# Another write pattern in a linear-attention readout, the first GLU opened tile by tile, and a new hand-written instruction order

## The chip, the cores and the metric

The kernel runs on one core of a Trainium2 chip. The metric is the device time of one execution in microseconds (us), as the median of several executions. A core has five engines with queues of their own: TensorE (PE in the profile, with its weight loads shown apart as PEld), VectorE (DVE), ScalarE (ACT), GpSimd (POOL) and SyncE (SP), which here only issues DMAs.

## What is computed

Four layers are applied to one sequence of 2048 tokens with 512 features, in bf16: attention A, GLU B, attention A, GLU B, each as `x = x + layer(layernorm(x))`, the two A layers with the same weights and the two B layers too. Cut to its core:

```python
def A(x, wqkv, w_phi, wo):                 # H = 32 heads of 16
    q, k, v = split_heads(x @ wqkv)
    pq, pk = q @ w_phi, k @ w_phi          # per head, 16 x 16
    phi_q = concat(softmax(pq), softmax(-pq))   # 32 features a head
    phi_k = concat(softmax(pk), softmax(-pk))
    kv = einsum("bhsf,bhsd->bhfd", phi_k, v)
    z  = einsum("bhsf->bhf", phi_k)
    num = einsum("bhqf,bhfd->bhqd", phi_q, kv)
    den = einsum("bhqf,bhf->bhq", phi_q, z)[..., None] + 1e-6
    return merge_heads(num / den) @ wo

def B(x, W_gate, W_up, W_down):            # F = 1376
    return (relu(x @ W_gate) * (x @ W_up)) @ W_down
```

## The kernel before

**Tiling.** The 2048 tokens are 16 tiles of 128 (`NT`), in four slabs of four. All weights and the whole of `x` stay in SBUF. `w_phi` is folded into the k and q weights at the start (`compose_k`, `compose_q`). The layers are called A0, B1, A2, B3 and the norms in front of them L0, L1, L2, L3.

**Attention.** For every tile, `kv_proj` or `kv_pair` (L670, L704) makes k and v and takes the exponentials. `knorm` (L689) sums them, takes the reciprocal and scales them. `kv_acc` (L721) adds `phi_k` times v into two banks of PSUM, with a column of ones beside each head's 16 values of v (`vsb[..., 16]`), so that z comes out in the same matmul. `kv_fin` (L737) copies the sums out with a mask: `kvf` for the feature-major readout, `kvbd` for the other.

**The two readouts.** In the first attention, tiles 0 to 3 have q in feature-major form (`q_fm`, L799), and `num_fm` (L813) reads them out. Eight matmuls a tile give the unnormalised result of both softmax signs, copies bring it to SBUF ("numcp"), and then come six small steps: `zm`, `zd`, `zr` (the reciprocal), `ab` (the factors), `tsc` (L845: all 1024 products) and `o` (L852: the sum of the two signs, 512 elements, written to `osb`). For tiles 0 and 1 the steps run on VectorE; for tiles 2 and 3 `zm`, `zd`, `ab` and `o` run on GpSimd. In `tsc` the order of a group's elements is feature, then head (`d h`); in `osb` it is head, then feature (`h d`), as the output projection wants it. All other tiles use `num` (L856), whose q goes through `qnorm` (L782) and two transposing DMAs.

**Behind the readout.** `out_proj` (L873) transposes `osb` (on PE for tiles 0 and 1, `PT`; by DMA for the others), multiplies by `wo`, and `resid` (L636) adds it to `x` with a running sum. `center` (L652) centres the tile for the next norm ("L1 apply") and transposes it ("L1 tr").

**GLU.** `glu_up` (L887) works on a list of tiles. It makes one piece for the last 96 of the 1376 hidden columns (`last`, "gu", L928, whose result goes through a transposing DMA, "htr") and ten pieces (`step`, L902) of 128 hidden columns: four matmuls for the gate, four for up, each with as many columns as the list has tokens. ScalarE takes the relu (L904); for some pieces it also copies up to SBUF (L910), and VectorE multiplies in SBUF (L912); for the others VectorE reads up from PSUM (L915). The pieces rotate through four banks of PSUM (0 to 3) and 18 places in `hT` (`NHU`). `glu_down` (L942) adds up a tile's eleven pieces and the residual (L953).

**What sets the order.** `emit` makes a list of all operations with what they read and write. `ORDER` gives for every engine the sequence in which it issues its operations, as positions in that list in base 36. Each engine runs its sequence strictly in that order and waits on semaphores where an operation needs another's result. `schedule` and `prepare` work out the waits from it; the duration that each operation carries in its call ("planner's duration") sets no wait on the chip by itself. SP's sequence holds nearly all DMAs, among them every transposing one.

Of the kernel before, what the change touches and what calls it, by code (L numbers as in the profile page):

```python
# [14 lines left out]
        "1i 1k 1j 1e 1h 1g 1f 1l 2e 47 2o 2y 3d 38 4r 3i 42 4c 4m 4w 3n 5n 5o 5b 67 66 5h 78 3s 7p 77 7o 91 92 6x 93 85 b8 b9 71 ba 8a cd ce a4 8f cf a8 8k di "  # L15
        "dj eb eh ec dk fb fc ei eo fd g9 ga en eu et gw gx la lb g8 gv lu hl hp lv il ip lk jl ll jp kd m5 m4 kh me mf mp mo o9 o8 nx ou ot oj p4 pe pf pp pz "
        "q0 qa if jf ql qk qv sw sx sl th t7 k7 kz ti uu ts v5 uv vf vg nm ws vq wt x3 z1 zd zc sa zn uj wh 110 zy zx 11b 11a 11l yi 11w 11v 12y 13j 139 138 "
        "10p 12n 178 14m 16x 16e 18a 17z 191 19c 19w 1ab 1b1 1a7 1bh 1cj 1bx 1an 1cl 1ck 1fj 1dl 1ax 1g8 1bd 1dj 1bt 1e9 1dk 1eb 1ea 1c9 1f0 1cx 1go 1ez 1f1 "
        "1hr 1h4 1gk 1jy 1g3 1hq 1hs 1ke 1ig 1if 1h0 1ku 1hg 1i4 1it 1iu 1ie 1la 1jh 1ju 1j6 1ji 1is 1ln 1lo 1ka 1kq 1mc 1jg 1mb 1l6 1lm 1n1 1n2 1m0 1ns 1ma "
        "1nr 1og 1n0 1oh 1ss 1sy 1pi 1pj 1nq 1to 1tn 1oj 1oi 1t4 1u2 1u1 1pl 1pk 1ta 1ug 1uf 1tm 1u0 1uu 1uv 1z0 1ue 1z1 1ut 1z2 1z3 1zf 1ze 1zd 1zo 1zc 1zp "  # L20
        "1zq 202 201 200 1zr 203 20d 20p 20o 20e 1wq 20r 20q 20c 20f 22a 22m 22b 21z 1xj 22w 22x 22l 1y4 238 237 1yp 23u 23i 23t 23j 24g 244 245 24f 24q 21o "
        "24r 251 252 275 276 26u 27h 26j 27g 27r 283 295 27s 282 296 29r 29h 29g 29s 2ad 2a3 2a2 2ae 2bh 2bg 2dt 2ds 2dh 28u 2ee 2b5 2e3 2e4 2ef 2eq 2ep 2ft "
        "2g3 2fs 2g4 2gf 2ge 2gq 2gp 2cy 2i3 2h0 2h1 2i4 2lm 2ly 2lx 2m8 2m9 2mk 2fh 2mv 2mu 2mj 2ny 2o8 2o9 2ok 2nx 2ou 2p6 2oj 2ov 2q8 2q9 2p5 2hs 2jl 2l3 "
        "2nm 2px 2rj 2ss 2t4 2t3 2tf 2tp 2te 2ub 2tq 2u0 2u1 2uc 2uy 2ux 2um 2un 2v9 2v8 2vv 2vj 2vk 2vu 2xp "),
    "dve": (
        "3x 25 26 2f 2g 29 4h 2p 2j 2q 2z 30 2t 33 4x 4z 4y 51 53 50 52 54 6j 6l 6k 6m 58 9r 9s 5p 5q 5e 68 69 6v 9t 9q 79 6z 7a 7q 7r 94 97 95 bb 98 a2 bc be "
        "bf cj a6 cg ck ch dl dm do dp fe fh ff gb fi gc gy ge gz mq h1 hf hb ha hd hc he hg hh hs ht hu hv hw hx is hy it iu iv i3 iw js ix i8 jv iy i9 jx j3 "
        "ie mr mx j8 j9 kk my je kn kp oa ny rl rm ok ov nc nd p5 k4 kw pg kx pq k5 s0 s1 qb tu q1 tv qm nj qw vs vt nk u9 r8 ua xt sm rk w7 w8 s7 s8 t8 sy tt "
        "tj ug xu uh 100 uw 101 v6 we wf vr vh wu 11y x4 11z 13x y8 13y y9 z2 zo 10f 15p ze 10g 15q 18c 18d 12d xg xs 12e 111 zz 17a 17b yf yg 10m 11c 14c 11m "
        "11x 14d 12z 10n 13k 12k 12l 13a 13w 164 165 14j 14k 150 17p 17q 15c 18r 18s 15o 16b 16c 19m 19n 16y 17w 1a9 18y 18z 17x 19t 19u 1fh 18b 179 1az 19d "  # L30
        "1g6 1a8 1ao 1bv 1bf 1be 1ay 1bu 1ca 1cy 1dm 1cm 1h2 1e0 1da 1jw 1cn 1ec 1ed 1g4 1gl 1gm 1ht 1dn 1hu 1f2 1eq 1hh 1kc 1ks 1h1 1f3 1ih 1ii 1fg 1l8 1i5 "
        "1j7 1iv 1iw 1jv 1kr 1kb 1lp 1jj 1lq 1l7 1jk 1md 1me 1m1 1n3 1n4 1nt 1mr 1nu 1sq 1ok 1nh 1ol 1sw 1pm 1pn 1o7 1t2 1tp 1or 1os 1p9 1t8 1tq 1u3 1u4 1pt "
        "1pu 1uh 1ui 1uk 1uw 1ux 1uz 1vy 1vz 1vw 1vx 20s 1w8 20t 1w9 20z 1x1 1we 210 1x2 1wj 1xu 1wk 1xv 1x7 1wp 1yf 1yg 1xc 1xd 21e 21f 1xi 285 25u 25v 220 "
        "1y1 1y2 1ym 22y 286 22c 22n 21l 21m 269 239 2ag 23v 1yn 23k 24h 26a 246 24s 2ah 253 28k 28l 25f 2es 2av 2aw 26v 26g 25s 27i 277 26h 28r 28s 2b2 284 "
        "2b3 27t 2et 297 29i 2c9 29t 2co 2af 2ca 2a4 2iw 2bi 2h3 2h4 2cp 2di 2du 2ke 2ix 2mx 2my 2f7 2f8 2eg 2kf 2bu 2er 2cv 2cw 2e5 2hi 2c7 2fu 2hj 2p8 2gg "
        "2fe 2ff 2gr 2g5 2p9 2jb 2jc 2hp 2hq 2h2 2i5 2ih 2kt 2ku 2ji 2jj 2ln 2kc 2lz 2iu 2nc 2nd 2ma 2pn 2po 2mw 2jz 2ml 2nj 2nk 2r9 2ra 2l0 2nz 2l1 2oa 2ol "
        "2ow 2qa 2p7 2qm 2pu 2pv 2rg 2rh 2st 2tg 2t5 2u2 2qz 2tr 2rx 2ud 2uo 2sa 2va 2uz 2vl 2vw 2w8 2wl 2wy 2xb 2xn "),
# [318 lines left out]
NT, NSLAB, NC, NFC = 16, 4, 4, 11  # L356
# [10 lines left out]
KVD = 31.0  # L367
# [6 lines left out]
class Kernel:  # L374
# [89 lines left out]
    def setup(self):  # L464
        op, dma, r = self.op, self.dma, self.r
        k = self
# [677 lines left out]
```

## Time and profile before

| what | value |
|---|---|
| median of six runs | 388.01 us |
| lowest and highest | 386.31 and 389.32 us |
| the profiled execution | 387.43 us |
| its span in the profile | 385.4 us |
| granted TensorE clock, mean over the span | 0.996 |
| instructions | 6623 |

The span is the time from the first to the last instruction that the profiler recorded; about 2.0 us of the profiled execution lie around it. In the profile a line such as L852 is a line of the kernel before. The word "busy" counts the time in which an engine has an instruction in work; matmuls overlap, so that a busy PE need not be one that streams at full rate. The chain that ended last is followed back from the last instruction, at each step to what released it.

### The profile page before, as it was taken

The page shows a single profiled execution, that of the slowest core. Times are in us where ns is not written, and L with a number is a line of the kernel's source. Part 1 is how long each engine was busy: PE and PEld are TensorE (multiplying, and loading weights), DVE is VectorE, ACT ScalarE, POOL GpSimd, SP SyncE. Part 2 cuts the span into 40 slices and gives each one's busy share as a digit, 9 for nine tenths or more (in the row PEclk, how much of TensorE's full clock was granted, in tenths as well). Part 3 has the DMA queues.
Part 4 walks back from the last instruction along what each step waited for, and adds up shares of the span by engine and source line. Part 5 has one row for each costly group of instructions (what it writes and reads, how often), then busy time and mean ns, then how long its engine had stood idle before and what let it go on. Part 6 is the DMA issues. An engine that isn't in the chain of part 4 may idle for free.

```text
span 385.4 us, 6623 instructions
## 1 busy us (share of the span) xinstructions
PE 366.8 (95%) x2416; PEld 200.1 (52%) x2459; DVE 260.9 (68%) x527; ACT 219.1 (57%) x433; POOL 161.4 (42%) x286
## 2 busy tenths in 40 slices
PE   5999987899999999999999999989999999999996
PEld 4555543576754445444444446566664444444443
DVE  4999889798868566346758697886766753441242
ACT  3899864753454307864656676975444623484540
POOL 7799932823354101713776777314037210103000
PEclk9999998999999999999999999999999999999999
DMA  7643950344535444400220124535534432231013
GB/s 244 155 81 59 281 227 0 70 80 97 89 66 84 96 95 84 82 3 0 56 41 0 25 44 58 83 69 82 79 73 97 82 80 57 71 69 41 2 27 123
DMA packets 92176, 30.37 MB, mean 79 GB/s; under 512 B 83984, under 2 KB 91120, under 8 KB 92144
## 3 DMA queue, kind: packets, MB, share of 16 engines
q1 hardware_dynamic: 90848, 28.84, 35.2%
q10 hardware_dynamic: 1296, 1.11, 1.0%
q8 instruction: 19, 0.31, 0.4%
q14 instruction: 13, 0.11, 0.1%
HBM read 7.91 MB, written 2.10 MB: 26 GB/s over the span
## 4 chain that ended last, share of the span: by engine, by line
PE 84%; DMA 5%; DVE 4%; ACT 3%; issue 1%; SPq 1%; ACTq 1%; POOL 1%; DVEq 0%
PE ps L902 35%; PE ps L951 18%; PE ps L677 9%; PE ps L882 7%; PE ps L711 4%; PE ps L767 3%; DMA oT<-osb 3%; PE ps L928 2%; PE ps L732 2%; DMA wv_p<-in_A_wqkv_dram 2%; PE ps L861 1%; ACT expq L772 1%; PE ps L807 1%; SPq L796 1%; DMA yT<-ytile 1%
## 5 line engine op out<-in xcount | busy, mean ns | idle before, releaser
L902 PE MATMUL ps<-yT,Wgu 128*128 128x512 bf16 (+1 forms) x788 | 148.0, 336 | 1.1 <-DVE h10t L933 0.5
L902 PEld LDWEIGHTS ps<-yT,Wgu 128*128 128x128 bf16 x800 | 75.6, 98 | 61.1 <-ACT expk L910 2.7
L904 ACT ACTIVATE gate_sb<-ps 128x512 bf16<-128x512 f32 (+1 forms) x100 | 49.6, 510 | 59.5 <-PE ps L902 34.7
L951 PE MATMUL ps<-Wd,hT 128*128 128x512 bf16 (+2 forms) x353 | 79.3, 372 | 0.6
L699 POOL TENSOR_TENSOR expk<-expk,rZk 128x1024 bf16<-128x1024 bf16 (+1 forms) x32 | 59.0, 1863 | 12.2 <-DVE rZk L694 12.2
L951 PEld LDWEIGHTS ps<-Wd,hT 128*128 128x128 bf16 (+1 forms) x363 | 34.8, 98 | 38.2 <-DMA hT<-h10t 0.5
L910 ACT ACTIVATE expk<-ps 128x512 bf16<-128x512 f32 (+1 forms) x65 | 32.0, 498 | 32.5 <-PE ps L902 30.1
L664 POOL TENSOR_SCALAR rv<-rv 128x1 f32<-128x1 f32 x48 | 8.8, 192 | 86.0 <-ACT sq L662 86.0
L912 DVE TENSOR_TENSOR hT<-gate_sb,expk 128x512 bf16<-128x512 bf16 (+1 forms) x65 | 24.8, 390 | 22.4 <-ACT gate_sb L904 14.3
L692 DVE TENSOR_REDUCE Zk<-expk 128x64 f32<-128x1024 bf16 x32 | 38.1, 1200 | 2.4 <-ACT expk L685 1.5
L915 DVE TENSOR_TENSOR hT<-gate_sb,ps 128x512 bf16<-128x512 bf16 (+1 forms) x35 | 20.9, 602 | 26.6 <-ACT gate_sb L904 14.8
L662 ACT ACTIVATE sq<-x_sb,nmr 128x512 bf16<-128x512 bf16 x48 | 34.6, 720 | 4.7 <-DVE x_sb L953 3.4
L785 DVE TENSOR_REDUCE Zq<-expq 128x64 f32<-128x1024 bf16 x28 | 33.7, 1205 | 4.4 <-ACT expq L772 2.9
L790 POOL TENSOR_TENSOR rho<-rZq,Zq 128x32 f32<-128x32 f32 x28 | 7.4, 267 | 68.9 <-DVE rZq L789 68.7
L953 DVE SCALAR_TENSOR_TENSOR x_sb<-ps,rstd,x_sb 128x512 bf16<-128x512 f32 (+1 forms) x33 | 23.4, 714 | 18.9 <-PE ps L951 15.3
L882 PE MATMUL ps<-wo_p,oT 128*128 128x512 bf16 x123 | 32.5, 386 | 3.3 <-DMA oT<-osb 2.5
L793 POOL TENSOR_TENSOR expq<-expq,rho 128x256 bf16<-128x256 bf16 x56 | 34.4, 629 | 1.6
L767 PE MATMUL ps<-Wqp,yT 128*128 128x512 bf16 x106 | 27.8, 386 | 0.5 <-issue 0.2
L639 DVE SCALAR_TENSOR_TENSOR x_sb<-ps,x_sb 128x512 bf16<-128x512 f32 x32 | 21.9, 685 | 7.5 <-PE ps L882 6.1
L677 PE MATMUL ps<-Wkp,yT 128*128 128x512 bf16 x86 | 22.6, 379 | 0.6 <-ACT Wkp L544 0.4
L868 DVE TENSOR_TENSOR osb<-ps,rden 128x512 bf16<-128x512 f32 x28 | 19.0, 680 | 5.2 <-DMA oT<-osb 4.7
L677 PE MATMUL ps<-wv_p,yT 128*128 128x512 bf16 x83 | 21.8, 379 | 0.8 <-DMA wv_p<-in_A_wqkv_dram 0.5
(116 smaller groups left out, 464.6 us busy)
## 6 DMA issues: line engine op xcount, KB each, us to landing
out_dram<-x_sb SPq DMA_DIRECT2D x15, 128.0 KB, 1.8
x_sb<-in_A_x_dram SPq DMA_DIRECT2D x3, 512.0 KB, 7.6
Wgu<-in_B_W_gate_dram SPq DMA_DIRECT2D x4, 344.0 KB, 6.6
Wgu<-in_B_W_up_dram SPq DMA_DIRECT2D x4, 344.0 KB, 6.6
Wd<-in_B_W_down_dram SPq DMA_DIRECT2D x5, 256.0 KB, 4.2
yT<-ytile SPq DMA_TRANSPOSE x56, 2.5
qT<-expq SPq DMA_TRANSPOSE x56, 2.5
x_sb<-in_A_x_dram SPq DMA_DIRECT2D x4, 128.0 KB, 3.6
```

What stands on the lines that cost most here:

```text
L662: op("act", lambda e: e.activation(k.sq[:], k.x_sb[:, t, :], ACT.Square, scale=-float(D), bias=k.nmr[:, t, :], accum_out=k.rv1[:, t, :]), ...
L677: op("pe", (lambda ic, bank, W: lambda e: e.matmul(k.pb[bank][:], k.yT[:, ic, t * 128:(t + 1) * 128], W[:, ic, :], start=(ic == 0), stop=( ...
L692: op("dve", lambda e: e.tensor_reduce(k.Zk[:, zb, :], k.expk[:, t, :, :, :].rearrange("p g s (h f) -> p (g s h) f", f=16), AX.X, ALU.add), ...
L699: op(eng, (lambda kv, u0, n: lambda e: e.tensor_tensor(kv, kv, k.rZk[:, rb, u0 * 32:u0 * 32 + n].unsqueeze(2).to_broadcast([P, n, 16]), AL ...
L767: op("pe", (lambda ic, bank, tt: lambda e: e.matmul(k.pb[bank][:], k.yT[:, ic, tt * 128:(tt + 1) * 128], k.Wqp[:, ic, :], start=(ic == 0), ...
L785: op("dve", lambda e: e.tensor_reduce(k.Zq[:, b, :], k.expq[:, t, :, :, :].rearrange("p g s (h f) -> p (g s h) f", f=16), AX.X, ALU.add), ...
L793: op("pool", (lambda ev, u: lambda e: e.tensor_tensor(ev, ev, k.rho[:, b, u * 16:u * 16 + 16].rearrange("p (g h) -> p g h", h=4).unsqueeze ...
L882: op("pe", (lambda c, bank: lambda e: e.matmul(k.pb[bank][:], k.oT[:, ob, c, :], k.wo_p[:, c, :], start=(c == 0), stop=(c == NC - 1)))(c, ...
L902: op("pe", (lambda bank, W, ic, fc, Mf: lambda e: e.matmul(k.pb[bank][0:Mf, 0:n], W[:, ic, fc * 128:fc * 128 + Mf], k.yT[:, ic, c0:c0 + n] ...
L904: op("act", (lambda Mf, gb, gs: lambda e: e.activation(k.gate_sb[0:Mf, gs, 0:n], k.pb[gb][0:Mf, 0:n], ACT.Relu))(Mf, gb, gs), [self.RP[gb] ...
L910: op("act", (lambda Mf, ub, up: lambda e: e.activation(up[0:Mf, 0:n], k.pb[ub][0:Mf, 0:n], ACT.Copy))(Mf, ub, up), [self.RP[ub]], ru, 170 ...
L951: op("pe", (lambda fc, Kf, u, c0, bank, m0, m1: lambda e: e.matmul(k.pb[bank][:, m0:m1], k.hT[0:Kf, u, c0:c0 + 128], k.Wd[0:Kf, fc, m0:m1] ...
```

## The change

Four things change in the code; the arithmetic stays the same.

1. The last add of the feature-major readout (`num_fm`, L850 to L852) goes through its elements in the order in which they lie in `osb`. It now writes neighbouring elements one after the other and reads both inputs at a step of 8 elements; before it read neighbouring elements and wrote at a step of 16.
2. In the first GLU, tiles 0 and 1 are worked on one after the other as lists of one tile each. Before they were one list of two. Tiles 2 and 3 stay a list of two, and the second GLU (`last`) is unchanged.
3. The column of ones in `vsb` is set by four fills, one for each slab, each with a resource of its own, instead of one fill.
4. All five sequences in `ORDER` are new, and some planner's durations.

```diff
-KVD = 31.0
+KVD = 33.0
...
-        op("pool", lambda e: e.memset(k.vsb[:, :, :, 16:17], 1.0), [], [r("vones")], 2270, "v ones")
+        for st in range(NSLAB):
+            op("pool", (lambda st: lambda e: e.memset(k.vsb[:, st * 4:st * 4 + 4, :, 16:17], 1.0))(st), [], [r("vones", st)], 620, f"v ones {st}")
...
-               [r("phik", t, bank), r("v", t), r("vones")], [self.RP[bank]], KVD, f"{tag} kvacc {t} {g}")
+               [r("phik", t, bank), r("v", t), r("vones", t // 4)], [self.RP[bank]], KVD, f"{tag} kvacc {t} {g}")
...
-        ov = k.osb[:, b, :].rearrange("p (c h d) -> p c d h", c=NC, h=8)
-        tv = k.tsc[b].rearrange("p (s c d h) -> p s c d h", s=2, c=NC, h=8)
+        ov = k.osb[:, b, :].rearrange("p (c h d) -> p c h d", c=NC, h=8)
+        tv = k.tsc[b].rearrange("p (s c d h) -> p s c h d", s=2, c=NC, h=8)
         op(sm, lambda e: e.tensor_tensor(ov, tv[:, 0], tv[:, 1], ALU.add),
-           [r("tsc", b)] + RT, [r("osb", b)], 600 if sm == "dve" else 1160, f"{tag} o {t}", port=135.0)
+           [r("tsc", b)] + RT, [r("osb", b)], 690 if sm == "dve" else 1200, f"{tag} o {t}", port=135.0)
...
-            mix(steps_B([0, 1], HA), steps_N([4]))
+            if last:
+                mix(steps_B([0, 1], HA), steps_N([4]))
+            else:
+                for f in steps_B([0], HA):
+                    f()
+                mix(steps_B([1], HA), steps_N([4]))
```

Counted by engine, PE issues 2539 operations instead of 2459, ScalarE 409 instead of 393, VectorE 490 instead of 479, GpSimd 285 instead of 282, and SP 194 instead of 193.

The sequences are too long to show. Read as names, they stand as follows at the places that matter here (a number behind a name is the tile, or the tile and the piece).

PE, from the end of the first attention's sums into the first GLU, before:

```
kvacc 15, num 0, q 6, num 1, q 7, num 1, q 12, num 2, otr 0, num 2, wo 0, q 10, num 3, q 11, otr 1, num 3, L1 tr 0,
q 13, wo 1, q 15, q 14, L1 tr 1, wo 2, [tiles 0 and 1:] Wu 0, Wg 0, gu 0, gu 1, Wu 1, Wu 2, Wg 2, Wg 1, num 4, ...
```

and after:

```
kvacc 15, q 8, num 0, q 7, num 1, q 6, num 2, q 12, q 13, num 2, otr 0, q 10, num 3, q 11, wo 0, num 3, otr 1, q 15, q 14,
L1 tr 0, num 4, wo 1, [tile 0:] Wu 0, Wg 0, gu 0, Wu 2, Wg 2, wo 2, Wg 1, Wu 1, Wg 4, L1 tr 1, Wg 3, Wu 3, Wu 4, ...,
wo 3, ..., gu 1, [tile 1:] Wu 1, Wg 0, num 5, Wg 1, num 5, Wu 0, down 0, Wg 2, ..., wo 4, ..., wo 5, down 1, gu 2, gu 3
```

VectorE over the same stretch, after:

```
kvf (four), kvbd (three), numcp 0, rZq 4, zm 0, kvbd, zd 0, zr 0, ab 0, numcp 1, zm 1, tsc 0, zd 1, zr 1, ab 1, o 0, tsc 1,
numcp 2, o 1, otr 0 copy, zr 2, tsc 2, resid 0, numcp 3, Zq 5, L1 apply 0, rZq 5, zr 3, otr 1 copy, L1 tr 0 copy, tsc 3, ...
```

SP behind the readout, after: `otr 2, otr 3, htr 0, qtr 5 (two), L1 tr 2, otr 4, qtr 6 (two), otr 5, htr 1, qtr 7, L1 tr 3`.

GpSimd at the start, before: `agg w0, mhalf, mone, kvf zero, agg w1, ones, mask8, ident, v ones, rv1 0`; after: `v ones 3, kvf zero, v ones 1, eps zero, ones, ident, mhalf, agg w0, mask8, agg w1, eps, v ones 2, v ones 0, rv1 0`. On ScalarE's queue the load of the last quarter of the k weights (`wk 3`) stands, after the change, behind the copy of another quarter's transpose (`wtrcopy wk 1`); before, it stood ahead of all copies.

## The prediction

> **What bounds the kernel now.** I read the page first, then the busy times by stretch, then the chain of work that ended last, then the groups by shape.
>
> ```profile
> span 385.4 us, 6623 instructions
> PE 366.8 (95%) x2416; PEld 200.1 (52%) x2459; DVE 260.9 (68%) x527; ACT 219.1 (57%) x433; POOL 161.4 (42%) x286
> ...
> PE   5999987899999999999999999989999999999996
> ...
> PEclk9999998999999999999999999999999999999999
> ```
>
> TensorE is the bound, and its only low stretches are the start, the last slice, and slices 6 to 8 (50 to 78 us), where the first layer passes from the numerators to the GLU. Some per cent of a time can only be won there, at the start, or at the end. The stretches say who is busy instead:
>
> ```profile
> core 0: us, PE busy (x) PEld busy (x) DVE busy (x) ACT busy (x) POOL busy (x), PEclk, DMA share, GB/s
> 50.00:60.00 10.00, 7.19 (x65) 4.13 (x64) 8.72 (x19) 7.22 (x12) 1.55 (x2) 1.00 0.39 150
> 60.00:70.00 10.00, 8.52 (x48) 4.31 (x50) 9.04 (x21) 5.11 (x8) 5.28 (x6) 0.83 0.01 2
> 70.00:80.00 10.00, 8.39 (x77) 6.51 (x76) 8.00 (x16) 5.98 (x13) 7.10 (x12) 1.00 0.43 85
> 80.00:90.00 10.00, 9.89 (x75) 6.36 (x76) 9.13 (x25) 3.73 (x11) 3.57 (x9) 1.00 0.55 93
> ```
>
> VectorE is the full one. From 60 to 70 us the granted clock falls to 0.83 besides (half speed for 3.4 us). The chain names the line:
>
> ```profile
> 58.28 0.06 DVE osb L852
> 58.34 1.79 issue
> ...
> 64.36 2.17 DVE osb L852
> ...
> 67.33 2.40 POOL osb L852
> ...
> 69.76 2.42 DMA oT<-osb
> ...
> 73.26 0.89 PE ps L902 x8
> ```
>
> L852 is the readout's last add, done twice on VectorE (tiles 0 and 1) and twice on GpSimd (2 and 3). Behind it stand the output projection, the layer norm, and the first GLU step, whose first matmul starts at 73.09 us in the timeline. The groups by shape give its price and its neighbours':
>
> ```profile
> L852 POOL TENSOR_TENSOR osb<-expk 128x512 bf16<-128x512 bf16 x2 | 4.8, 2393 | 1.9 <-DVE expk L845 1.9
> L852 DVE TENSOR_TENSOR osb<-expk 128x512 bf16<-128x512 bf16 x2 | 4.6, 2280 | 0.0
> L845 DVE TENSOR_TENSOR expk<-expk,hT 128x1024 bf16<-128x1024 bf16 x4 | 2.7, 684 | 0.5 <-POOL hT L841 0.5
> L915 DVE TENSOR_TENSOR hT<-gate_sb,ps 128x512 bf16<-128x512 bf16 x25 | 16.9, 681 | 25.1 <-ACT gate_sb L904 14.8 <-PE ps L902 7.8 <-PE ps L861 2.4
> ```
>
> The add of 512 takes 2.28 us, 3.3 times its neighbour of 1024 elements. GpSimd is idle at 58.2 us, so this is not a wait for it: the pattern costs it.
>
> **How much is lost there.** Pitches of back-to-back matmuls, from the chain and the timeline: 512 columns 0.216 us (four in 0.86), 256 columns 0.109 (twenty in 2.18), 192 columns 0.083 (sixteen in 1.32), 68 columns 0.033; by interpolation 0.063 for 144 and 0.056 for 128. From the last kvacc (52.85) to the first GLU matmul (73.09) PE does eight q projections (6.9 us), 32 feature-major numerators (2.0), three output projections (2.6) and four transposes (0.9): 12.4 us of work in 20.2, so 7.8 lost, 1.7 of it by the half clock. The same count over the rest finds about 10 us lost before 20 us, 0.7 more up to 82 us, 3 us after PE's end, and some 4 us scattered elsewhere.
>
> **The add (L852).** New: it writes in order and reads both inputs at a step of 8 elements (16 bytes); old: it reads in order and writes at a step of 16 elements (32 bytes). No row reads SBUF at such a step. Bounds on VectorE: 0.44 us (512 elements, fast mode, L912) and 2.28 us or above (if the read pays what the write paid). Rows with a strided read lie low: L753 reads PSUM 17 fp32 apart, 272 elements in 439 ns against 136 in 294 for L742, 1.07 ns per element more and nothing else. I take the one-element-per-cycle row, 0.68 us (L915): 1.6 us less, twice. GpSimd: between 1.25 us (two L793 adds of 256 at 629 ns) and 2.4; I take 1.3.
>
> [...] The trace shows a write that steps 32 bytes at 2.28 us. [...]
>
> **The chain re-added.** New VectorE order from 53.02, start-to-start times from the same trace: four kvf 1.88, three kvbd 0.63, copy 0.45, rZq 0.30, zm 0.26, kvbd 0.22, zd 0.23, zr 0.39, ab 0.26, copy 0.37, zm 1 0.26, tsc 0 0.61, zd 1, zr 1, ab 1 0.88, o 0 0.62, tsc 1 0.61, copy 0.37, o 1 0.60: o 1 is done at about 62.0, not 66.5. Then the transpose's copy 0.35, zr 2 (GpSimd's zm 2 and zd 2 end at 62.4) until 62.9, tsc 2 (ab 2 first) until 64.0, resid 0 0.7, copy 0.4, Zq 5 1.13, L1 apply 0 0.4: 66.7. PE: transpose 0.25, four numerators, wo 1 (its copy is ready at 67.7): the GLU begins near 68.6, because tile 0 alone suffices. That is 4.5 us earlier, but wo 2 and one transpose, less four numerators (0.96 us), are still to be done: 3.5 us won. With no idle stretch as long as the 1.8 us at 58.4 I expect the half-clock time to go; that is inside the 3.5. About 4.3 us stays lost, because VectorE's chain is still longer than PE's work.
>
> **GLU tile by tile.** Tiles 0 and 1 of the first GLU: 80 matmuls of 256 columns (8.7 us) become 160 of 128 (160 x 0.056 = 9.0): +0.2. ScalarE gets 16 instructions more: 256 columns 383 ns, 512 columns 595, so 128 about 277; two for one +0.17, some 2.7 us, beside 3.7 to 6.0 busy of 10. VectorE: 128 columns about 278 (SBUF) or 267 ns (PSUM); two for one +0.22 and +0.13, eleven times, about 2.0 us, against 3.2 saved. If ScalarE's cover were gone, its 2.7 us would fall on PE. One more transposing DMA goes through SP (1.24 us of issue). L1 tr 3 stands behind it, L1 tr 2, three otr and three qtr; counted from apply 2 (74.1), it lands near 86 to 87, when PE wants it (GLU 2, 3). That cover is thin: 0.3 us charged.
> PSUM turnaround: an up bank read by VectorE is held 0.22 (fill) + 0.20 + 0.28 (relu) + 0.05 + 0.28 + 0.06 = 1.09 us, and is wanted again after two steps, 0.88 us of PE. The other work between them (two wo, down 0, numerators) covers most; I charge 0.5 us.
>
> **Ones per slab, and the start.** One fill of 2.27 us becomes four of about 0.6 on GpSimd; two of them, the kvf fill (1.06) and one of 0.2 now stand ahead of `ones` and `ident`, so `ident` comes near 3.7 us instead of 2.64. The first transposes started at 3.54 on a DMA: 0 to 0.2 lost, hidden until the wv landing at 9.48. Without that cover it is 1 us. The two slabs ahead of rv1 0 end near 5.6, where rv1 0 began at 5.52. On ScalarE's queue the load of wk 3 now stands behind a copy that waits for PE's transposes: issued near 7.2 instead of 4.13, landed near 10.5, wanted at 11.6. Nothing.
>
> **The new order elsewhere.** From 20 to 52 us PE loses nothing and VectorE is 90 to 98% busy, and after 90 us little is lost: I set 0, with -1.5 to +2 as bounds, since no row prices an order.
>
> **Sum.** -3.5 + 0.2 + 0.3 + 0.5 = -2.5, and of the scattered 0.7 up to 82 us some 0.5 goes with the add: -3.0. The profiled execution took 387.43 (span 385.4 and 2.0 around it): 384.4. The median of the six is 388.01, 0.6 above it: **385.0**.
>
> **Rivals.**
> - The reads pay (20%). The add stays at 2.28 us: the VectorE chain is 3.2 us longer, the GLU begins at 71.8, 0.3 is won and spent on the turnaround: 388.0. For: the old price is itself a stride's. Against: L753.
> - The small steps become the bound (10%), slower. The ten odd steps of tiles 0 and 1 wait for VectorE, which stands behind a 1.2 us reduction or a 0.77 us residual, 89% full by its own sum (30.4 us of instructions in 34). At 0.6 us each that is 6 us lost, 2.5 over the gain: 390.5. It decides from 0.35 us a step. For: VectorE at 9.13 of 10 from 80 to 90. Against: the 256-column steps lose 0.2 us there.
> - More is won (5%): PE idles little before the GLU and most of the 8.5 us comes back: 381.5.
>
> **How the numbers follow.** The forecast has 65%, 383 to 387 on its own bounds. With the rivals' 388.0 inside, and the order's +-1.5, the range is 382.0 to 388.6. Half a per cent is 1.9 us, about what a measurement of this kernel tells from no change: faster means below 386.1. Of the forecast's 65% some 59 lie below, the 5% too; the first rival and the forecast's rest are "same"; of the last 10%, 8 lie above 389.9.
>
> **What would show it.** Right: L852 on VectorE near 0.68 us and on GpSimd near 1.3; the first L902 matmul near 68.6 us; granted clock 1.00 from 60 to 70; PE's slices 6 to 8 fuller. Wrong: L852 above 1.5 us; L902 loads of 128-column steps waiting for DVE h; `yT<-ytile` ending a PE wait near 87 us; a first v projection much later than 9.5 us.

## The result, and the profile after

The kernel after takes 390.22 us (median of 20 runs, 388.69 to 392.31) where the kernel before takes 387.43 (41 runs). The ratio is 1.0070, 95% interval 1.0054 to 1.0086: 2.8 us slower, not 3 us faster. The profiled execution took 391.23 us, against 387.43 before. In the new file everything around the change stands five lines lower: L852 is now L857, L902 is L907, L928 is L933, L861 is L866.

First the page of after.

```profile
span 389.4 us, 6827 instructions
PE 368.9 (95%) x2496; PEld 200.1 (51%) x2539; DVE 259.5 (67%) x538; ACT 221.4 (57%) x449; POOL 161.1 (41%) x289
...
PE   5999988999999999999999999899899997999995
...
PEclk9999999999999999999999999999999998999999
...
q8 instruction: 20, 0.33, 0.4%
```

The hole that the forecast aimed at is nearly closed: slices 6 to 8 (50 to 78 us) read 8, 8, 9. New holes stand far behind it: a 7 in slice 34 (321 to 331 us), where the granted clock falls too, and an 8 in slice 29 (273 to 282 us). The page of before has 9 in both places. (The 8 in slice 26 has a counterpart in before, in slice 27.)

The stretches around the change:

```profile
core 0: us, PE busy (x) PEld busy (x) DVE busy (x) ACT busy (x) POOL busy (x), PEclk, DMA share, GB/s
50.00:60.00 10.00, 8.64 (x92) 4.98 (x92) 8.67 (x23) 6.47 (x11) 3.25 (x5) 1.00 0.34 113
60.00:70.00 10.00, 8.22 (x65) 4.63 (x65) 8.58 (x19) 8.71 (x14) 5.66 (x8) 1.00 0.61 151
70.00:80.00 10.00, 9.69 (x124) 7.32 (x125) 9.23 (x29) 6.50 (x25) 4.30 (x9) 1.00 0.49 70
80.00:90.00 10.00, 9.95 (x109) 7.25 (x109) 8.51 (x23) 4.03 (x15) 3.15 (x9) 1.00 0.49 86
```

The clock is 1.00 from 60 to 70 us (0.83 before), and TensorE is fuller from 50 to 60 and from 70 to 80. The add itself, from the groups by shape:

```profile
L857 POOL TENSOR_TENSOR osb<-expk 128x512 bf16<-128x512 bf16 x2 | 4.2, 2114 | 1.7 <-DVE expk L850 1.7
...
L857 DVE TENSOR_TENSOR osb<-expk 128x512 bf16<-128x512 bf16 x2 | 2.2, 1077 | 0.0
```

It fell from 2280 to 1077 ns on VectorE, and from 2393 to only 2114 on GpSimd. The timeline (start, duration, engine, line) has the first GLU matmul at 69.17 us, 3.9 earlier than before:

```profile
69.17 0.61 PE L907 MATMUL ps<-yT,Wgu 128*128 128x128 bf16 x8
```

**A count of what TensorE loses.** I added the pitches of all matmuls but the 44 on `ones` at the start, which feed nothing (the pitches of the prediction), and took them from the time that had passed. In the kernel before 18.6 us are lost at 90 us, in the kernel after 15.9: the first layer gained 2.7. At 100 us it is 18.6 against 17.0. At TensorE's end it is 22.4 against 25.6. So 4.8 us were given back behind 100 us, and 0.8 more of the profiled difference lies behind TensorE's end.

TensorE's waits from 200 to 340 us in the kernel after (us in total, times, longest) say at what:

```profile
PE ps L866 <- DMA qT<-expq: 2.5, 2, 2.3
PE ps L933 <- DMA yT<-ytile: 1.7, 2, 1.5
PE ps L887 <- DMA oT<-osb: 1.1, 1, 1.1
```

All three are transposing DMAs. The same stretch of before has only an oT wait of 1.4 and a yT wait of 0.4. The chain of after (start, length, what) around the longest one:

```profile
319.58 0.58 SPq L968
...
320.20 4.30 DMA qT<-expq
...
324.55 0.30 PE ps L866 x4
```

This DMA is one half of qT of tile 13. SP issues it at 320.20 us; it takes 4.30 us to land, and PE stands for 2.3 of them. The view of the tile qT from 300 to 330 us gives least, median and longest landing; first before, then after:

```profile
DMA to landing us min/median/max: 2.4/2.5/2.5
```

```profile
DMA to landing us min/median/max: 2.5/2.8/4.3
```

Two stretches of after show what it cost; before they had 9.54 and 9.95 of PE, at clock 1.00:

```profile
280.00:290.00 10.00, 8.27 (x60) 4.79 (x59) 5.57 (x10) 3.36 (x10) 1.66 (x4) 1.00 0.26 29
320.00:330.00 10.00, 7.63 (x51) 4.18 (x51) 2.53 (x5) 2.39 (x6) 0.00 (x0) 0.83 0.58 110
```

Behind the 2.3 us of idleness the granted clock is 0.5 for 3.41 us, so another 1.7 us go: 4.2 us are lost between 320 and 330 us, and 2.0 between 280 and 290.

### The profile page after: what moved, and what is told of

Its sections match the earlier page's. It is cut to its first block, busy times and chain, and to the rows that moved or that the text cites. A ratio compares the mean times of both kernels' runs of the same rounds, so it can differ in the third digit from the quotient of the medians.

```text
span 389.4 us, 6827 instructions
## 1 busy us (share of the span) xinstructions
PE 368.9 (95%) x2496; PEld 200.1 (51%) x2539; DVE 259.5 (67%) x538; ACT 221.4 (57%) x449; POOL 161.1 (41%) x289
## 4 chain that ended last, share of the span: by engine, by line
PE 80%; DMA 8%; ACT 4%; DVE 4%; SPq 1%; issue 1%; POOL 1%; DVEq 0%; ACTq 0%; POOLq 0%
PE ps L907 34%; PE ps L956 17%; PE ps L682 8%; PE ps L887 6%; PE ps L772 4%; DMA qT<-expq 3%; PE ps L716 3%; PE ps L737 2%; PE ps L933 2%; PE ps L866 2%; DMA yT<-ytile 2%; DMA oT<-osb 1%; DMA x_sb<-in_A_x_dram 1%; ACT expk L719 1%; PE ps L812 1%
## 5 line engine op out<-in xcount | busy, mean ns | idle before, releaser
L907 PE MATMUL ps<-yT,Wgu 128*128 128x512 bf16 (+2 forms) x865 | 150.8, 322 | 0.9
L907 PEld LDWEIGHTS ps<-yT,Wgu 128*128 128x128 bf16 x880 | 77.6, 98 | 61.4 <-ACT gate_sb L909 2.6
L909 ACT ACTIVATE gate_sb<-ps 128x512 bf16<-128x512 f32 (+2 forms) x110 | 51.3, 482 | 57.3 <-PE ps L907 46.6
L915 ACT ACTIVATE expk<-ps 128x512 bf16<-128x512 f32 (+2 forms) x70 | 32.4, 475 | 32.9 <-PE ps L907 29.8
L917 DVE TENSOR_TENSOR hT<-gate_sb,expk 128x512 bf16<-128x512 bf16 (+2 forms) x70 | 24.1, 360 | 36.2 <-ACT gate_sb L909 22.7
L887 PE MATMUL ps<-wo_p,oT 128*128 128x512 bf16 x120 | 31.0, 379 | 2.5 <-DMA oT<-osb 1.1
L920 DVE TENSOR_TENSOR hT<-gate_sb,ps 128x512 bf16<-128x512 bf16 (+2 forms) x40 | 21.5, 546 | 16.2 <-ACT gate_sb L909 9.1
L872 DVE RECIPROCAL rden<-ps 128x32 f32<-128x32 f32 x28 | 9.8, 352 | 17.7 <-PE ps L866 17.5
```

The lines of the kernel that those rows point to most:

```text
L887: op("pe", (lambda c, bank: lambda e: e.matmul(k.pb[bank][:], k.oT[:, ob, c, :], k.wo_p[:, c, :], start=(c == 0), stop=(c == NC - 1)))(c, ...
L907: op("pe", (lambda bank, W, ic, fc, Mf: lambda e: e.matmul(k.pb[bank][0:Mf, 0:n], W[:, ic, fc * 128:fc * 128 + Mf], k.yT[:, ic, c0:c0 + n] ...
L909: op("act", (lambda Mf, gb, gs: lambda e: e.activation(k.gate_sb[0:Mf, gs, 0:n], k.pb[gb][0:Mf, 0:n], ACT.Relu))(Mf, gb, gs), [self.RP[gb] ...
L915: op("act", (lambda Mf, ub, up: lambda e: e.activation(up[0:Mf, 0:n], k.pb[ub][0:Mf, 0:n], ACT.Copy))(Mf, ub, up), [self.RP[ub]], ru, 170 ...
```

## The experiments

Ratios are to the kernel before, timed on the same chip beside each kernel. "First half" means the sequences up to about 120 us, "second half" those from there on.

**1. The add alone.** The kernel before, with only the new order of the add's elements.

```diff
-        ov = ...rearrange("p (c h d) -> p c d h", ...)
-        tv = ...rearrange("p (s c d h) -> p s c d h", ...)
+        ov = ...rearrange("p (c h d) -> p c h d", ...)
+        tv = ...rearrange("p (s c d h) -> p s c h d", ...)
```

> The kernel before with the new element order of the last readout add (L850 to L852) and nothing else: the sequences and the GLU stay. Theory A (the change's own parts win at the readout what was forecast there, and two transposing DMAs that land late in the second layer lose it again): the add takes 1.08 us as in the profile after, 1.2 us less twice on VectorE's chain, so the first GLU matmul comes about 2.4 us earlier than 73.1 and the half-clock time near 62 us shrinks or goes: 385.0, 2.0 to 3.0 below the kernel before. Theory B (the parts themselves do not pay, since VectorE or the queue of transposing DMAs takes the gain back within the next stages): within 0.7 of the kernel before.

Measured: 385.0 us, ratio 0.9946 (0.9924 to 0.9969). That is 2.1 us faster, from two lines. Its stretches:

```profile
50.00:60.00 10.00, 7.88 (x73) 4.51 (x71) 8.69 (x22) 7.22 (x12) 2.06 (x2) 1.00 0.47 183
60.00:70.00 10.00, 8.51 (x58) 4.26 (x57) 8.77 (x22) 7.71 (x10) 6.80 (x12) 1.00 0.10 20
70.00:80.00 10.00, 9.01 (x87) 7.43 (x87) 8.38 (x17) 4.68 (x13) 4.37 (x6) 1.00 0.43 87
```

The half clock of 60 to 70 us is gone, the first GLU matmul starts at 70.34 us, and TensorE has lost 16.4 us at 100 us: less than the kernel after (17.0), whose GLU opens 1.2 us earlier. So the add is the gain, and the other parts of the change, put on top of it, lose more than it brings.

**2. Everything but the add.** The kernel after with the old order of the add's elements (the diff above, backwards).

> The kernel after with the old element order of the last readout add and nothing else undone. Theory A: VectorE's chain to the first GLU matmul is 2.4 us longer, that matmul moves from 69.2 to about 71.6; the late DMAs of the second layer stay, so the time is 392 to 393, 2 to 2.5 above the kernel after. Theory B: within 0.7 of the kernel after.

Measured: 393.12 us, ratio 1.0164 (1.0123 to 1.0205). The first GLU matmul starts at 72.33 us. In these sequences the new add is worth 0.0094, some 3.6 us; in the old ones 2.1, and the intervals don't tell the two apart. The rest of the change alone costs 6.4 us by this ratio.

**3. What the add's step costs.** Ten adds of 128x512 bf16 elements with steps `s`, each twice on VectorE and twice on GpSimd, stand at the end of the kernel before; one of them is shown. The time of the whole isn't used.

```diff
+        vs = lambda T, t, s: full(T, t)[:, 0:512 * s].rearrange("p (n s) -> p n s", s=s)[:, :, 0]
...
+            lambda e: e.tensor_tensor(z(1), x(8), y(8), ALU.add),
...
```

> The kernel before with forty more adds of 128x512 bf16 at its end, on tiles no longer used, twenty on VectorE and then twenty on GpSimd, so that its own time is not compared: each reads two inputs and writes one output with a step of 1, 2, 4, 8 or 16 elements. [...] On GpSimd both inputs at 8 elements cost 2.1 us, at 1 about 1.2.

The lines 1086 to 1095 have these steps, in elements of 2 bytes, of first input, second input and output: 1 1 1; 2 2 1; 4 4 1; 8 8 1; 16 16 1; 8 1 1; 1 1 2; 1 1 4; 1 1 8; 1 1 16. The groups by shape (the last number before the second bar is the mean in ns):

```profile
L1094 POOL TENSOR_TENSOR expk<-expk,expq 128x512 bf16<-128x512 bf16 x2 | 4.9, 2456 | 0.2
L1094 DVE TENSOR_TENSOR expk<-expk,expq 128x512 bf16<-128x512 bf16 x2 | 4.8, 2422 | 0.1
...
L1095 DVE TENSOR_TENSOR expk<-expk,expq 128x512 bf16<-128x512 bf16 x2 | 4.6, 2296 | 0.1
...
L1089 POOL TENSOR_TENSOR expk<-expk,expq 128x512 bf16<-128x512 bf16 x2 | 4.2, 2102 | 0.2
...
L1088 POOL TENSOR_TENSOR expk<-expk,expq 128x512 bf16<-128x512 bf16 x2 | 3.0, 1485 | 0.2
...
L1093 POOL TENSOR_TENSOR expk<-expk,expq 128x512 bf16<-128x512 bf16 x2 | 2.7, 1328 | 0.2
L1093 DVE TENSOR_TENSOR expk<-expk,expq 128x512 bf16<-128x512 bf16 x2 | 2.6, 1294 | 0.1
...
L1090 DVE TENSOR_TENSOR expk<-expk,expq 128x512 bf16<-128x512 bf16 x2 | 2.1, 1075 | 0.1
L1089 DVE TENSOR_TENSOR expk<-expk,expq 128x512 bf16<-128x512 bf16 x2 | 2.1, 1056 | 0.1
L1091 DVE TENSOR_TENSOR expk<-expk,expq 128x512 bf16<-128x512 bf16 x2 | 2.1, 1052 | 0.1
L1092 DVE TENSOR_TENSOR expk<-expk,expq 128x512 bf16<-128x512 bf16 x2 | 1.5, 730 | 0.1
L1087 DVE TENSOR_TENSOR expk<-expk,expq 128x512 bf16<-128x512 bf16 x2 | 1.4, 692 | 0.1
L1088 DVE TENSOR_TENSOR expk<-expk,expq 128x512 bf16<-128x512 bf16 x2 | 1.4, 692 | 0.1
...
L1086 DVE TENSOR_TENSOR expk<-expk,expq 128x512 bf16<-128x512 bf16 x2 | 0.8, 420 | 0.0
```

Read on VectorE: in order 420 ns; 692 at 4 and at 8 bytes, near the row that the forecast took (0.68); 1056 at 16 bytes, and much the same where one input alone steps (1052) and at 32 bytes (1075). Write at a step: 730 at 4 bytes, 1294 at 8, about 2300 to 2400 at 16 and 32. So the change traded a write of about 2.3 us for a read of 1.06, which is 0.36 above that at a step of 4 or 8 bytes. GpSimd reads at 16 bytes for 2102 ns and at 8 for 1485.

**4. Both adds of tiles 2 and 3 on VectorE too,** from the add alone.

```diff
-        op(sm, lambda e: e.tensor_tensor(ov, tv[:, 0], tv[:, 1], ALU.add),
+        op("dve", lambda e: e.tensor_tensor(ov, tv[:, 0], tv[:, 1], ALU.add),
```

In VectorE's sequence each now stands behind its `tsc`.

> The kernel before with the new add, and the adds of tiles 2 and 3 on VectorE too (behind their tsc) instead of GpSimd. An add of 1.05 us takes the place of one of 2.11, so oT of tiles 2 and 3 lands about 1 us earlier, but VectorE gets 2.1 us more where it is 87 to 90 per cent busy. If GpSimd's add is on the path: 384 to 384.5; if VectorE's load is: 385.5 to 386.5; the add alone took 385.0 (ratio 0.9946).

Measured: 384.31 us, ratio 0.9932 (0.9906 to 0.9958): the fastest kernel here, with all four adds at 1052 ns. The interval overlaps that of the add alone, so the second step's own worth is not shown.

**5. The halves of the sequences, swapped.** To learn where the order loses, two kernels take one half from each. Kernel X is the kernel after with every engine's sequence from about 120 us on taken from before; kernel Y is the kernel before with the new add, and the sequences of after from there on. Two lines behind the first list of tiles keep the places and banks that the later sequence was made for:

```diff
+            if not last:
+                self.unit += 7
+                next(gring), next(gring)
```

(in kernel Y `self.unit += NFC`). Kernel X:

> The kernel after up to about 120 us (start, new add, tiles 0 and 1 of the first GLU one by one, all five sequences), and from there on the sequences of the kernel before (places and banks of the later pieces are numbered as before). Theory (the first part of the change gains, the new sequences of the second half lose): at 100 us TensorE has lost 1.7 to 2.7 us less than in the kernel before, and nothing is given back, so 384.5 to 385.5, ratio to before 0.993 to 0.996. Rival (the opening tile by tile or the new start costs later, wherever the sequences come from): 388 to 390, ratio above 1.002.

Kernel Y:

> The kernel before with the new add up to about 120 us, and from there on the sequences of the kernel after. Theory (the new sequences of the second half cost some 5 us by themselves): 389 to 391, ratio to before 1.005 to 1.010. Rival (those sequences cost only where TensorE's instruction fetches happen to fall on a transposing DMA; this kernel issues 160 fewer matmuls ahead of them than the kernel after, so the fetches fall elsewhere): no wait of 2 us near 320 us, 386 to 387.5, ratio 0.998 to 1.001.

With the add alone and the kernel after this makes a square:

| first half | second half of before | second half of after |
|---|---|---|
| before, new add | 0.9946 (0.9924 to 0.9969) | 1.0043 (1.0017 to 1.0068) |
| after | 0.9979 (0.9950 to 1.0008) | 1.0070 (1.0054 to 1.0086) |

The new second half costs 0.0097 in the upper row and 0.0091 in the lower one: 3.8 and 3.5 us of 387.4. The new first half (tiles 0 and 1 one by one, ones by slab, new start and order) costs 1.3 and 1.0 us, each within what these intervals leave open. Both ways through the square agree, so the halves simply add up: -2.1 for the add, +1.2 for the new first half, +3.6 for the new second half make the +2.7 of the kernel after. Kernel X missed its window (0.993 to 0.996) and stayed below the rival's 1.002; kernel Y missed its by little. In kernel Y the very same SP sequence puts the same half of qT at 320.1 us, and it lands in 2.40; PE waits 1.0 us for it. So the stall of 2.3 us is no fixed property of that sequence, but a loss of 3.8 us was there all the same.

**6. What makes a transposing DMA late.** On one DMA queue, q8, the page counts 20 packets of kind "instruction" and 0.33 MB (16384 bytes each in the trace); before had 19. Their starts in the trace lie about 125 matmuls (97 to 171 in before and after), or 250 instructions with the weight loads, apart, and PE has 80 matmuls and 80 weight loads more now. I read them as TensorE's program being fetched, though the trace doesn't name their engine; waits put ahead of that program move them (below). The DMA view of after from 320 to 325 us (packets, MB, share; then issues with median landing):

```profile
q8 instruction: 1, 0.02, 1.4%
...
qT<-expq SPq DMA_TRANSPOSE x3, 3.6
```

and of kernel Y over the same 5 us, where the fetch falls elsewhere and no line for q8 appears:

```profile
q1 hardware_dynamic: 1843, 0.53, 48.0%
...
qT<-expq SPq DMA_TRANSPOSE x3, 2.5
```

Over the traces of before, after and eleven of these kernels (all but the price run) I counted all 1957 transposing DMAs (but for the one of the weights at each start). Of 377 that had such a fetch starting between issue and landing, or at work at issue, 298 landed later than 2.75 us; of the other 1580, 54 did. Where the fetch starts on the way, the median landing is 3.82 us; without, 2.48. A longer flight has more room for a fetch, but that isn't it: of the DMAs with a fetch starting 0.3 to 2.1 us after issue, all 188 landed late. The half of qT of tile 13 took 4.30, 4.1 and 3.15 us in the three kernels where a fetch lay on it (after, number 2, and the 32 waits below), and 2.4 to 2.6 in the ten others.

Two kernels move the fetches. Waits on GpSimd's first operation, fulfilled before PE has work, stand ahead of PE's first operation, 64 or 32 of them:

```diff
+        if e == "pe":
+            for _ in range(64):
+                eng.wait_ge(sems["pool"], 1)
         for o in self.per_engine_seq[e]:
```

> The kernel after with 64 more waits at the head of TensorE's queue, each already fulfilled when TensorE needs nothing yet; they move the places at which TensorE's instructions are fetched. Theory A, with the fetch as the cause of the late landings: the fetches near 279.5 and 322.3 us move by some 5 us, the transposing DMAs of 278.5 and 320.2 land in 2.5 us, TensorE's waits of 1.5 and 2.3 us and the half clock behind the second go, and unless other transposes that TensorE waits for are hit the time is 386 to 388. A rival, that the sequence of SP is late by itself: the waits stay and the time is 390.2 within 0.7, or more by the time of the 64 waits.

> The kernel after with 32 more waits at the head of TensorE's queue instead of 64, so that they are over before TensorE has work and cost nothing at the start. The fetches of TensorE's instructions come 16 matmuls earlier in its program. Theory A with the fetch as the cause: the wait near 324 us shrinks by 1 us or more and the half clock behind it goes in most runs: 387 to 389, unless another transposing DMA that TensorE waits for is hit. The rival that the sequence of SP is late by itself: 390.2 within 0.7.

With 64 the ratio is 1.0098 (1.0060 to 1.0136), and the waits themselves cost 1.1 us at the start; with 32 it is 1.0070 (1.0051 to 1.0090), as without any. In both profiles the loss of 320 to 330 us shrank, from 4.2 to 1.4 and 1.2 us, and other waits grew. In the one with 64, from 200 to 340 us:

```profile
PE ps L890 <- DMA oT<-osb: 1.9, 2, 1.2
PE ps L936 <- DMA yT<-ytile: 1.7, 2, 0.9
PE ps L869 <- DMA qT<-expq: 1.1, 1, 1.1
```

The expectation of a gain failed for both; in time the rival's 390.2 came closer, though the waits did move. With 32 the profiled execution is the fastest of its six (387.79, median 389.25) and its waits sum to 3.6 us instead of 5.3, so it doesn't show what the others lost; the DMAs of its three longest waits have a fetch on them (3.2 to 3.5 us to land).

With 64, all five DMAs that PE waits for land in 2.4 to 2.5 us. But each stands on SP's queue behind another transposing DMA whose issue a fetch met. That issue took SP 2.2 to 2.7 us instead of 1.27, and SP had no pause in between to catch up: half of qT of tile 13 is issued at 322.60, behind one issued at 319.64 that took 2.29, as the chain of that kernel shows:

```profile
319.64 2.29 SPq L668
...
322.60 2.39 DMA qT<-expq
```

So it is with this half in kernel Y, behind an issue of 2.40 at 313.07. Over the thirteen traces, 1720 issues of transposing DMAs that no fetch overlaps took 1.26 us in the median and at most 1.58; of the 237 that one overlaps, 121 took more than 1.6. In these traces a fetch thus delays the transposing DMA that is on its way (3.82 us to land against 2.48, in the median) and those queued behind an issue that it overlaps (here 2.29 us long, against 1.26).

**7. SP's sequence around the late ones.** First tile 13's half of qT goes ahead, in the kernel after:

```diff
-SP: ... otr 11, otr 10, L3 tr 8, qtr 15, qtr 14, L3 tr 9, L3 tr 10, L3 tr 11, store 5, qtr 13
+SP: ... otr 11, otr 10, qtr 13, L3 tr 8, qtr 15, qtr 14, L3 tr 9, L3 tr 10, L3 tr 11, store 5
```

> The kernel after with one transposing DMA (the first half of q of tile 13 in the second attention layer) issued five places earlier in SP's sequence, where SP idles; nothing else. Theory A: TensorE's wait of 2.3 us at 324 us and the half clock behind it (3.4 us at half speed, 1.7 us) go: 386.2, 4 below the kernel after, in every run near the runs that kept the clock. The rival that TensorE has another wait just behind it: 388 to 390.

Measured: 387.32 us, ratio 1.0004 (0.9981 to 1.0026), 0.0066 below the kernel after (2.6 us), between Theory A's 386.2 and the rival's 388. The loss of 320 to 330 us is 0.6. In its profiled execution, the slowest of twelve (389.88), the clock now halves behind the other wait, of 1.5 us for yT:

```profile
280.00:290.00 10.00, 8.02 (x54) 4.99 (x53) 4.29 (x10) 2.92 (x9) 0.34 (x2) 0.83 0.27 32
```

Then L3 tr 6 and 7 go ahead of a half of qT that is wanted later:

```diff
-SP: ... L3 tr 5, qtr 11, L3 tr 6, L3 tr 7, htr 2
+SP: ... L3 tr 5, L3 tr 6, L3 tr 7, qtr 11, htr 2
```

> The kernel after with two changes in SP's sequence: the transposing DMA of the first half of q of tile 13 five places earlier (as in the run before), and the one of a half of q of tile 11 behind those of L3 tr 6 and L3 tr 7 instead of in front of them, so that these two start 1.25 us earlier. Theory A (late transposing DMAs in the second layer): the 1.5 us wait near 282 us falls to 0.3 to 0.8 us, the clock stays at 1.00 from 270 to 330 us, and the time is 385.5 to 386.5, below the kernel before. Theory B (the change's own parts lose): 387.3, as with the one DMA moved.

Measured: 386.36 us, ratio 1.0005 (0.9987 to 1.0024). No further gain in the ratio: it isn't below the kernel before, as Theory A had it. The wait near 283 us fell to 1.2 us only, not to 0.3 to 0.8, and no half clock stands from 270 to 330 us. Last, both moves in kernel Y:

> The kernel before with the new add up to about 120 us, the sequences of the kernel after from there on (1.0043 so far), and in SP's sequence the same two transposing DMAs moved as in the run with both stalls taken away (one half of tile 13's qT ahead of L3 tr 8, one half of tile 11's behind L3 tr 6 and 7). Theory (what the new second half costs is the place of these two on SP's queue): ratio to before 0.995 to 0.998, as with the add alone (0.9946). Rival (the rest of the new second half costs too): 1.000 to 1.003, and in the profile the waits above 0.5 us from 200 to 340 us stand at other lines than the two moved ones.

Measured: 386.85 us, ratio 1.0005 (0.9983 to 1.0027), as the rival had it. Of the 0.0097 that the second half costs, 0.0038 was these two places, give or take 0.0034. The largest wait that remains is for a third DMA of the same kind, here otr 7, with a fetch beside it (the waits from 200 to 340 us, then the DMA view from 271 to 276):

```profile
PE ps L882 <- DMA oT<-osb: 3.0, 2, 1.9
```

```profile
q8 instruction: 1, 0.02, 1.7%
...
oT<-osb SPq DMA_TRANSPOSE x1, 4.3
```

TensorE's waits for transposing DMAs from 200 to 340 us, summed: with before's second half 1.8 us (before), 1.6 (number 1), 1.3 (number 4) and 1.4 (X, whose first half holds as many PE instructions as that of the kernel after); with the new one 5.3 (after), 5.5, 4.7, 3.9, 3.0, 3.9, 3.6, 3.8 and 3.0 in all eight variants of it. Wherever the fetches fell, the new second half had a DMA with too little time in hand.

Another part of the second half's cost has nothing to do with them. From the end of PE's last matmul to the end of the span it is 3.2 us in the four kernels with before's second half and 3.8 to 4.25 in all nine with the new one. The last store, from ScalarE's queue, lands 2.1 to 2.4 us after its issue there instead of 1.7; why is not known.

**8. The pair again, in the kernel after.** Tiles 0 and 1 of the first GLU are one list of two, in sequences otherwise as near to the new ones as they could be kept.

```diff
-                for f in steps_B([0], HA):
-                    f()
-                mix(steps_B([1], HA), steps_N([4]))
+                mix(steps_B([0, 1], HA), steps_N([4]))
```

The two lines of number 5 (`self.unit += NFC`) stand here too, and PE's and the other sequences lose tile 1's pieces.

> The kernel after with the first GLU's tiles 0 and 1 again as one list of two: tile 1's pieces are dropped from the sequences, L1 tr 1 and wo 2 stand in front of the first piece, everything else keeps its place. If opening tile by tile pays, the GLU begins at about 71.7 instead of 69.2 us with 1.1 us more work done before it, and TensorE has lost 1 to 1.5 us more by 90 us. If the small steps cost what they win (two tiles of ten steps with more instructions on ScalarE and VectorE), the loss by 100 us is the same within 0.4. The time of the whole moves with the places of the instruction fetches (160 TensorE instructions fewer) and says less: 386 to 391.

Measured: 396.25 us, ratio 1.0256 (1.0233 to 1.0280), far above what was expected. The first GLU matmul starts at 73.19 us, and TensorE loses 23.5 us up to 100 us instead of 17.0:

```profile
60.00:70.00 10.00, 8.23 (x56) 4.14 (x55) 8.79 (x19) 9.15 (x14) 4.79 (x8) 1.00 0.79 156
70.00:80.00 10.00, 8.03 (x68) 6.28 (x69) 6.04 (x14) 4.10 (x12) 3.50 (x5) 1.00 0.23 45
80.00:90.00 10.00, 7.91 (x61) 4.71 (x61) 7.73 (x20) 4.31 (x12) 3.57 (x8) 1.00 0.40 56
```

This sequence brings tile 1 late and needs the opening with tile 0 alone. So the run doesn't tell the worth of that opening in a sequence made for a pair: in the kernel with the add alone, which has such a sequence, the GLU began 1.2 us later and no more was lost by 100 us.

## Why the prediction was wrong

**The step that failed is "The new order elsewhere".** It was set at 0 with bounds of -1.5 to +2; in the second half alone it cost 3.5 to 3.8 us (number 5), and that is more than all of the 2.8 us by which the kernel is slower. The reason given was that little is lost behind 90 us. That is a fact about the old sequence, and tells nothing of how little time a new one leaves its DMAs. Of SP's sequence the prediction followed the front name by name, the rest not. There half of qT of tile 13 moves from ahead of L3 tr 11 to behind it and a store, from 310.6 us to 320.2; PE is ready for it at 322.2 (its matmul at 324.55 less the wait of 2.3), sooner than even a landing in 2.5 us would be.

From the forecast's -3.0 to the measured +2.8 it is 5.8 us. The second half is 3.6 of them. The other 2.2 lie in the first half: kernel X, which has the whole change up to about 120 us, is 0.8 us faster than before by its ratio (from 1.9 faster to 0.3 slower), not 3.0. There -4.0 was set for the add and the earlier opening together and 1.0 charged; the add brings 2.1, and the rest of the first half costs 1.0 to 1.3.

**What went right.**
- The VectorE chain: the second add was to end at 62.0 us and ends at 62.4 (with luck: each add took 0.4 us longer than forecast, and the chain began at 52.67, 0.35 earlier); the GLU was to begin near 68.6 and begins at 69.17; the half clock of 60 to 70 us is gone (1.00 there). 3.0 us less were to be lost behind the opening, and at 90 us of the profiled execution it is 2.7.
- GLU tile by tile: 1.0 us was charged; from 70 to 90 us TensorE loses 0.8 for all reasons, and none of its longer waits is for the small steps. The rival "the small steps become the bound" is refuted; that its 390.5 lies so near the 390.2 measured is chance, since slower came by another mechanism.
- The start: nothing lost (9.5 us by 20 us, 9.95 before), though PE's first wait is 3.3 us now instead of 2.2.

**What was mis-sized.** The add: 1.08 and 2.11 us against 0.68 and 1.3. The 0.68 us is the time of L915 (681 ns for 512 elements, 405 for 256: 1.08 ns an element), and the 0.44 that of L912 (440 and 332 ns: 0.42 an element); that the one takes an element a cycle, and that the other is a mode of its own, no run shows. The PSUM row (L753, 1.07 ns an element) that was put against the rival "the reads pay" doesn't speak for SBUF, where number 3 has 692 ns for the add at a read step of 8 bytes and 1056 at 16. But the add didn't stay at 2.28 us, as that rival had it, since the old write (2280 ns) was dearer than any read (1075 at most in number 3). The write costs 1294 ns already at a step of 8 bytes. "The reads pay" was thus half right. And what is left of the 3.5 us credited to the add and the new opening together is the add's: alone, in the old order, it brings 2.2 us by 100 us and 2.1 in the median.

**What stays open.** Whether a sequence with the new opening could keep the 1.2 us by which its GLU starts earlier: X has it with the old second half, and is not faster than the add alone. Where in the first half its 1.0 to 1.3 us go isn't settled either, and the intervals allow nothing at all. By the count above, TensorE loses 1.1 us from 20 to 50 us in the kernel after and 0.9 in X, where before and number 1 lose nothing (the forecast had "From 20 to 52 us PE loses nothing" of the old order); the start wins some of that back, and a wait of 0.8 us for qT stands near 92 us. Four of the eleven executions of X behind its ratio also have a mean clock of 0.996 or less, as one stretch at half clock gives (3.41 us at 0.5 in some 384; median 388.3 us, the others 385.7); the one profiled is not among them. And why a fetch delays transposing DMAs is not shown, only that it does.

## What to carry to other kernels

Judge a new instruction order by the time that each transfer has in hand before its reader, not by how little the old order lost; read the whole sequence of the queue that issues the transfers, and leave each critical one the slack of its late case. Try a local repair such as a better write pattern alone, before it is bundled with a new order: here two lines gave 0.5%, and the bundle took it back. Where an add of this form on VectorE must step by 8, 16 or 32 bytes, let the reads step and the writes run in order (692, 1056 and 1075 ns against 1294, 2422 and 2296); on GpSimd that held at 16 bytes (2102 against 2456 ns) but not at 8 (1485 against 1328).

## What the runs showed of the hardware

- Transposing DMAs landed in 2.48 us in the median, and in 3.82 where a packet that I read as a fetch of TensorE's instructions (16384 bytes; 0.9 to 1.6 us long in before and after, about 1.1 in the median) started while they were on their way; in the kernel with 64 waits SP's issues that met one took 2.2 to 2.7 us, against 1.26 for those without. The kernel after, with 2539 matmuls and as many weight loads, has 20 such fetches, and which transfers they hit moves with the instructions ahead: 32 waits moved one from 322.3 to 320.1 us.
- The granted clock fell to one half for 3.41 us behind an idle stretch of TensorE of 2.3 us, in the kernel with tile 13's half moved ahead (number 7) behind one of 1.5 us, and in kernel Y with both moves it stayed at 1.00 behind one of 1.9. In the kernel after, 16 of 21 executions with a recorded clock have a mean clock of 0.998 or less, with a median of 391.0 us; the five others have 388.9, still above the 387.4 of the kernel before.
- Strided adds of 512 bf16 elements on VectorE: reads 692 ns at a step of 4 and of 8 bytes, 1056 at 16 and 1075 at 32; writes 730, 1294, 2422 and 2296 ns at 4, 8, 16 and 32 bytes.
